# Attention grouped by half batches, and half of one batch's queries turned by the DMA

## The chip, the cores and the metric

The kernel runs on one core of a Trainium2 chip. The metric is the device time of one execution in microseconds. Engines are called by their names: TensorE (PE in the profile) multiplies matrices, VectorE (DVE) and ScalarE (ACT) work on tiles elementwise, GpSimd (POOL) and SyncE (SP) issue DMAs here.

## The reference

Linformer attention for 8 batches, 8 heads, 1024 tokens and head size 64, with keys and values projected to 64 rows, and then a maxout layer of two products on the 8192 tokens:

```python
k_proj = np.einsum('ks,bhsd->bhkd', E, k)
v_proj = np.einsum('ks,bhsd->bhkd', F, v)
scores = scale * np.matmul(q, k_proj.transpose(0, 1, 3, 2))
scores = scores - np.max(scores, axis=-1, keepdims=True)
attn = np.exp(scores)
attn = attn / (np.sum(attn, axis=-1, keepdims=True) + 1e-09)
attn_out = np.matmul(attn, v_proj)
x = attn_out.transpose(0, 2, 1, 3).reshape(B * S, H * D)
h1 = x @ w1
h2 = x @ w2
g = np.maximum(h1, h2)
return (g @ w_out).astype(np.float32)
```

w1 and w2 are 512x1024, w_out is 1024x512.

## The kernel before

**Units.** A unit is half a batch: 512 tokens, all 512 features; there are two for each of 8 batches, numbered n = 0 to 15 in the order in which they are done. The layer on a unit has up products (L745: x times a difference of weights, then a relu on the result, the tile gt_sb) and down products (L837: gt_sb and x times output weights). Both are made with seven block products in place of eight, so VectorE forms sums of blocks first (L705, the tiles that the profile calls big). In the main loop the seven up products of unit n+1 (p1, p2, p6, p5, p7, p3, p4, for two passes d = 0 and 1) alternate on TensorE with pieces of the down products of unit n. ScalarE copies most results out of their bank (`keep`, L719), and VectorE adds others (L760), then takes the relu (L763).

**The order** is written out by hand. A list `slots` holds the matmul pieces with keys, and `at_slot(key, step, ...)` puts further work behind one of them: `("P", n, p, i)` is piece i of down product p of unit n; `("U", n, h, i)` is up product i of half h of unit n (h is the pass d); `("G", n, h)` is the place at the head of half h. Each engine works through its instructions in the order in which the loop emits them.

**Attention** of a batch is done in four groups: two halves of the tokens (j) times two groups of four heads (g). A group has scores (16 small matmuls on tiles of 64x32, L340), their exp (ScalarE, into ex_sb), sums of the exps (8 matmuls by ones, L352) and values (16 matmuls, L352), the log and the exp of minus the log of the sums (ScalarE, ld_sb: the inverse), and the product of values and inverse (VectorE, into xt_sb, which is x of the layer). In the steady state `step_group` at `("G", n, h)` does the scores of the next group into banks mm2 and mm3, then sums and values of the group before (`step_da`) in the two double banks called att. The exps (two of 128x512), the log, the inverse and one product of 128x1024 (L499) follow in that half of the unit, so each half of a unit has one product. `step_later` puts log, inverse and product into slots `U(n, h, 0)` to `U(n, h, 2)`.

The sums of the exps are tested once per inverse: `check` (L396) lets SP write a few rows of ld_sb to a tile.

**Batch 1** is started in the down products of unit 0, by a string of names with one slot each: kv and kpt are projections of k and v, qt00 to qt11 turn q on TensorE (8 transposes each, L311, with a copy out by VectorE, L316), sc00 and sc10 are scores, dn and in sums and inverses, at and AT values and products. The key `("P", n // 15, (n - 1) // 2 % 7, (n - 1) % 2)` maps the place in the string to a piece.

**Later batches** have their q turned by DMA_TRANSPOSE from SP (`step_qt_dma`, L323) in two halves by heads. `step_gate` makes GpSimd's next loads wait for it. Batch 2 has its projections of k and v in unit 1 (`step_kv_sets`, `step_kpt_sets`), batches 3 to 7 in the units n = 3, 5, 7, 9 and 11 (`kv_units`; `step_kv` at `G(n, 0)`, L195, with the copies L205 to L212 by VectorE).

Of the kernel before, what the change touches and what calls it, by code (L numbers as in the profile page):

```python
# [19 lines left out]
def kernel(  # L20
# [12 lines left out]
    nc = tc.nc  # L33
# [272 lines left out]
    def step_qt(t, h0, nh=2, i0=0, i1=NI, att=False):  # L306
        qt_ps = att_banks(FP16)[:, 0, :] if att else mm_bank(FP16)
        ni = i1 - i0
        for h in range(nh):
            for i in range(ni):  # L310
                nc.tensor.transpose(  # L311
                    out=qt_ps[:, (h * ni + i) * 128 : (h * ni + i + 1) * 128],
                    in_=t["q"][:, h0 + h, 2 * (i0 + i) : 2 * (i0 + i) + 2, :],
                    identity=ident16,
                )
        nc.vector.tensor_copy(  # L316
            out=t["qt"][:, h0 : h0 + nh, i0 * 128 : i1 * 128],
            in_=qt_ps[:, 0 : nh * ni * 128].rearrange("q (h n) -> q h n", h=nh),
        )


    def step_qt_dma(t, h0=0, h1=H):
        nc.sync.dma_start_transpose(  # L323
# [6 lines left out]
    W = HALF // 2  # L330
    Z = D // 2

    def score(t, g, j, banks):
        for h in range(2):
            for o in range(2):
                for e in range(2):
                    head = 4 * g + 2 * h + e
                    for s in range(2):
                        pos = D * (o ^ e) + s * Z
                        nc.tensor.matmul(  # L340
                            out=banks[e][pos : pos + Z, h * W : (h + 1) * W],
                            lhsT=kpt_of(t, head, o)[:, s * Z : (s + 1) * Z],
                            rhs=t["qt"][o * D : (o + 1) * D, head, j * W : (j + 1) * W],
                            start=True, stop=True,
                        )
        t["ex", g, j] = soft.tile([128, 2, HALF], FP16, tag="soft", name="ex_sb")
# [24 lines left out]

    def x_out(t, g, j):
        return t["xt"][:, 2 * g : 2 * g + 2, :, j * W : (j + 1) * W]
# [74 lines left out]
            )  # L448


    def step_group(ln_later, t, g, j, t2, g2, j2):
        def new():
            if t is None:
                return lambda: None
            banks = [mm_bank(n=2 + e) for e in range(2)]
            score(t, g, j, banks)
            return lambda: scores(t, g, j, banks)

        if t2 is None:
            new()()  # L460
            t_later[0] = None
        else:
            first = (g, j) == (0, 0) and t is not tiles[2]
            acts = None if first else new()
            t_later[0] = step_da(t2, g2, j2, lambda: (new() if first else acts)(), ln_later)

    def scores(t, g, j, banks):
        for e in t["first"]:
            nc.scalar.activation(  # L469
                out=t["ex", g, j][:, e, :], in_=banks[e], func=ACTF.Exp, scale=scale  # L470
            )

    t_later = [None]

    def step_later():
        if t_later[0] is not None:
            t_later[0] = t_later[0]()

    def step_da(t, g, j, between, ln_later):
        if "xt" not in t:  # L480
            new_xt(t)
        dn_ps = att_banks()[:, :, 0:W]
        at_ps = att_banks()
        sums_into(t, g, j, dn_ps)
        values_into(t, g, j, [at_ps[:, o, :] for o in range(2)])
        between()
        ld = soft.tile([128, 2, W], FP32, tag="soft", name="ld_sb")

        def ln():
            nc.scalar.activation(out=ld, in_=dn_ps, func=ACTF.Ln)  # L490
            return invert

        def invert():
            nc.scalar.activation(out=ld, in_=ld, func=ACTF.Exp, scale=-1.0)
            check(ld)
            return finish

        def finish():
            nc.vector.tensor_tensor(  # L499
                out=x_out(t, g, j).rearrange("q z o n -> q o z n"),  # L500
                in0=at_ps.rearrange("q o (z n) -> q o z n", z=2),
                in1=ld[:, :, None, :].broadcast_to([128, 2, 2, W]),
                op=ALU.mult,
            )

        return ln if ln_later else ln()

# [505 lines left out]
    def loads(b, *names):  # L1013
        for n in names:
            b_ = b + (n == "k" and b < 2)
            if (b_, n) == (1, "q"):
                alloc(tiles[1], "q")
                for c in (0, NC // 2):
                    nc.gpsimd.dma_start(
                        out=tiles[1]["q"][:, :, c : c + NC // 2],  # L1020
                        in_=q[1].rearrange("h (p c) d -> p h c d", c=NC)[:, :, c : c + NC // 2],
                    )
# [59 lines left out]
    at_slot((0, 22), new_attn, t)  # L1082
    at_slot((0, 22), lambda: turn.__setitem__(slice(None), [2, 3]))
    for n, x in enumerate((
        "", "", "", "", "", "kv", "", "kpt", "qt00 qt10", "", "sc00 sc10", "qt01",
        "qt11 dn00 in00 dn10 in10", "", "", "at00 AT10 sc01",
    )):
        key = ("P", n // 15, (n - 1) // 2 % 7, (n - 1) % 2) if n else (0, 22)
        for name in x.split():
            if name[0] == "k":  # L1090
                if name == "kpt":
                    at_slot(key, step_kpt_sets, t)
                else:
                    at_slot(key, step_kv_sets, t)
                    at_slot(key, loads, 2, "v", "q")
            else:
                g, j = int(name[2]), int(name[3])
                s_ = {"qt": step_qt, "sc": step_sc,
                      "dn": step_dn, "in": step_inv, "at": step_at, "AT": step_at}[name[:2]]
                args = (4 * g, 4, 2 * j, 2 * j + 2) if name[:2] == "qt" else (g, j)  # L1100
                at_slot(key, s_, t, *args, *([True] if name[:2] == "AT" else []))
        if n in (1, 5):
            at_slot(key, step_t, 1, (0, 1) if n == 1 else (2, 3))
        if n in (2, 3):
            for i in range(2):
                at_slot(key, step_tw, 2 * (n - 2) + i)
        if 6 <= n < 10:
            at_slot(key, sums_x, U[0, 1], ((2, 0, 1, 3)[n - 6],))
# [1 line left out]

    t = tiles[2]
    at_slot(("P", 0, 2, 0), new_attn, t)
    at_slot(("P", 0, 2, 0), step_qt_dma, t, 0, H // 2)
    at_slot(("U", 1, 0, 1), step_kv_sets, t)
    at_slot(("U", 1, 0, 4), step_kpt_sets, t)
    at_slot(("P", 0, 6, 0), step_qt_dma, t, H // 2, H)
    at_slot(("U", 1, 0, 6), step_gate, t, "qt", H // 2 - 1)
    at_slot(("U", 1, 0, 6), loads, 3, "k", "v", "q")
# [12 lines left out]
        at_slot(("U", n, 0, 6), loads, b + 1, "k", "v", "q")  # L1131
    for n, h in (3, 1), (4, 0), (4, 1), (5, 1), (6, 0), (6, 1), (7, 1), (8, 0):
        at_slot(("U", n, h, 3), lambda: held.pop(0)())
    groups = [(tiles[b], g, j) for b in range(1, B) for j in range(2) for g in range(2)][2:]
    none = (None, None, None)
    for i, (new, old) in enumerate(zip([*groups[1:], none], groups)):
        n, h = divmod(i + 2, 2)
        if new[0] is not None:
            at_slot(("G", n, h), lambda t=new[0], h=h: t.__setitem__("first", (h, 1 - h)))
        ln_later = (n, h) == (1, 1) or h == 0 and n in kv_units  # L1140
        at_slot(("G", n, h), step_group, ln_later, *new, *old)
        at_slot(("U", n, h, 0), step_later)
        if ln_later:
            at_slot(("U", n, h, 1), step_later)
        at_slot(("U", n, h, 2), step_later)

    for n, (b, o) in enumerate(units):
        u = U[b, o]
# [215 lines left out]
```

## Time and profile before

| | |
|---|---|
| median of 3 runs | 320.2 us (320.08 to 320.25) |
| profiled execution: span | 318.1 us |
| profiled execution: time | about 320.2 us, some 2.1 us of it around the span |
| granted TensorE clock | 1.000 |
| TensorE busy | 312.3 us, 3922 matmuls |
| VectorE busy | 241.1 us, 441 instructions |
| ScalarE busy | 206.2 us, 373 instructions |
| HBM read, written | 57.15 MB, 16.78 MB |

In a row of the timeline the first number is the start in us after the start of the span, the second how long the instruction (or the x instructions of the row, which overlap) took; matmuls are pipelined, so the time from one start to the next is what one costs. In brackets stands for how long the engine had been idle and what ended that. A row of waits has the total in us, the number of times and the longest. In the lists of 40 digits each digit is the busy share of 1/40 of the span in tenths.

### The profile page before, as it was taken

The numbers are of one execution on the slowest core, as the hardware profiler recorded it, in microseconds if no ns is written. First come the engines' busy times: TensorE is split into PE (matmuls) and PEld (weight loads), VectorE is DVE, ScalarE is ACT, GpSimd is POOL, SyncE is SP. The second block draws the span as 40 slices with busy tenths as digits, with TensorE's granted clock in tenths as the row PEclk, the third lists the DMA queues.
The fourth block names the chain that finished last, engine by engine and source line by source line (L and its number), as shares of the span: only waits on it lengthen the run. The fifth ranks groups of instructions, "written<-read, shape, count | busy, mean of one in ns | idle before, by whom it ended". The sixth has DMA issues, their size and how long they took to land.

```text
span 318.1 us, 9308 instructions
## 1 busy us (share of the span) xinstructions
PE 312.3 (98%) x3922; PEld 253.6 (80%) x3922; DVE 241.1 (76%) x441; ACT 206.2 (65%) x373; POOL 40.8 (13%) x63
## 2 busy tenths in 40 slices
PE   8989999999999999999999999999999999999996
PEld 3555588888887888788887888788887888888885
DVE  2366888877969696996969696996969696969883
ACT  2476842777776777477776778477776777765541
POOL 8259002003000300022000400030000000000000
PEclk9999999999999999999999999999999999999999
DMA  7999999999979999899999999989979131313124
GB/s 189 206 200 195 207 206 202 207 158 160 204 139 195 162 212 245 210 182 154 223 233 217 167 204 245 215 151 183 232 149 209 45 102 36 102 35 102 36 99 136
DMA packets 76684, 53.71 MB, mean 169 GB/s; under 512 B 29664, under 2 KB 76128, under 8 KB 76640
## 3 DMA queue, kind: packets, MB, share of 16 engines
q0 software_dynamic: 30688, 28.05, 56.0%
q1 hardware_dynamic: 45664, 24.85, 32.7%
q8 instruction: 31, 0.51, 0.6%
q10 hardware_dynamic: 288, 0.20, 0.2%
q14 instruction: 13, 0.11, 0.1%
HBM read 57.15 MB, written 16.78 MB: 232 GB/s over the span
## 4 chain that ended last, share of the span: by engine, by line
PE 92%; DMA 5%; POOL 1%; ACT 1%; issue 0%; DVE 0%; POOLq 0%
PE mm_ps L837 47%; PE mm_ps L745 27%; PE mm_ps L524 4%; DMA v_sb<-in_v_dram 4%; PE att_ps L352 3%; PE mm_ps L195 3%; PE mm_ps L340 2%; PE mm_ps L633 2%; PE att_ps L237 1%; DMA out_dram<-o_sb 1%; PE mm_ps L311 1%; POOL k_sb L108 0%; POOL q_sb L108 0%; ACT ld_sb L388 0%; ACT ex_sb L380 0%
## 5 line engine op out<-in xcount | busy, mean ns | idle before, releaser
L719 ACT COPY p_sb<-mm_ps 128x512 f32<-128x512 f32 x179 | 101.8, 592 | 49.1 <-PE mm_ps L745 27.2
L837 PEld LDWEIGHTS <-big 128*128 128x128 f16 x768 | 73.5, 98 | 11.8 <-issue 3.6
L837 PE MATMUL mm_ps<-T_sb,big 128*128 128x256 f16 x576 | 76.9, 273 | 0.0
L760 DVE TENSOR_TENSOR gt_sb<-mm_ps,p_sb 128x512 f16<-128x512 f32 x56 | 38.5, 687 | 43.0 <-PE mm_ps L745 41.6
L745 PE MATMUL mm_ps<-big,big 128*128 128x256 f16 x336 | 50.4, 273 | 0.0
L745 PEld LDWEIGHTS <-big 128*128 128x128 f16 x448 | 43.8, 98 | 5.1
L837 PE MATMUL mm_ps<-wo_sb,gt_sb 128*128 128x256 f16 x256 | 42.6, 273 | 0.0
L837 PEld LDWEIGHTS <-gt_sb 128*128 128x128 f16 x376 | 35.7, 98 | 6.7 <-issue 2.7
L469 ACT ACTIVATE ex_sb<-mm_ps 128x512 f16<-128x512 f32 x50 | 27.2, 596 | 18.0 <-PE mm_ps L340 12.3
L745 PEld LDWEIGHTS <-wd_sb 128*128 128x128 f16 x336 | 32.9, 98 | 3.8
L745 PE MATMUL mm_ps<-xt_sb,wd_sb 128*128 128x256 f16 x224 | 32.8, 273 | 0.0
L499 DVE TENSOR_TENSOR xt_sb<-att_ps,ld_sb 128x1024 f16<-128x1024 f32 x26 | 31.7, 1219 | 0.2
L837 PE MATMUL mm_ps<-m_sb,xt_sb 128*128 128x256 f16 x128 | 24.4, 273 | 0.0
L303 POOL COPY junk<-qt_sb 1x1 f16<-1x1 f16 x6 | 2.1, 346 | 172.5 <-DMA qt_sb<-q_sb 172.5
L868 DVE TENSOR_TENSOR o_sb<-mm_ps,p_sb 128x512 f32<-128x512 f32 x32 | 21.9, 683 | 2.8 <-ACT p_sb L897 2.0
L763 DVE TENSOR_SCALAR gt_sb<-gt_sb 128x512 f16<-128x512 f16 (+1 forms) x60 | 20.9, 348 | 2.1
L705 DVE TENSOR_TENSOR big<-gt_sb 128x1024 f16<-128x1024 f16 x32 | 21.8, 683 | 0.0
L837 PE MATMUL mm_ps<-wo_sb,big 128*128 128x256 f16 x128 | 21.5, 273 | 0.0
L806 ACT ACTIVATE gt_sb<-mm_ps 128x512 f16<-128x512 f32 x28 | 16.8, 601 | 5.7 <-PE mm_ps L745 5.7
L837 PE MATMUL mm_ps<-T_sb,gt_sb 128*128 128x256 f16 x120 | 20.3, 273 | 0.0
L837 PEld LDWEIGHTS <-xt_sb 128*128 128x128 f16 x188 | 18.3, 98 | 2.3 <-issue 0.2
L760 DVE TENSOR_TENSOR gt_sb<-p_sb 128x512 f16<-128x512 f32 x28 | 19.1, 682 | 0.6 <-ACT p_sb L719 0.6
(121 smaller groups left out, 434.7 us busy)
## 6 DMA issues: line engine op xcount, KB each, us to landing
out_dram<-o_sb SPq DMA_DIRECT2D x62, 256.0 KB
k_sb<-in_k_dram POOLq DMA_DIRECT2D x7, 1024.0 KB, 9.8
v_sb<-in_v_dram POOLq DMA_DIRECT2D x7, 1024.0 KB, 15.3
q_sb<-in_q_dram POOLq DMA_DIRECT2D x5, 1024.0 KB, 23.0
q_sb<-in_q_dram POOLq DMA_DIRECT2D x6, 512.0 KB, 15.8
big<-in_moe_w_dram POOLq DMA_DIRECT2D x12, 128.0 KB, 6.3
v_sb<-in_v_dram POOLq DMA_DIRECT2D x4, 256.0 KB, 13.6
wo_sb<-in_moe_w_out_dram POOLq DMA_DIRECT2D x1, 1024.0 KB, 10.4
```

What stands on the lines that cost most here:

```text
L195: nc.tensor.matmul(out=kv_ps[r * KP : (r + 1) * KP, h * D : (h + nh) * D], lhsT=eft[i][:, c, :], rhs=t[w][:, h0 + h : h0 + h + nh, c, :], ...
L469: nc.scalar.activation(out=t["ex", g, j][:, e, :], in_=banks[e], func=ACTF.Exp, scale=scale)
L499: nc.vector.tensor_tensor(out=x_out(t, g, j).rearrange("q z o n -> q o z n"), in0=at_ps.rearrange("q o (z n) -> q o z n", z=2), in1=ld[:, ...
L524: nc.tensor.matmul(out=h_ps, lhsT=wd_sb[:, r, fb * 128 : (fb + 1) * 128], rhs=t["xt"][:, r, :, j * W : (j + 1) * W], start=(r == 0), stop= ...
L705: nc.vector.tensor_tensor(out=S(i), in0=S(0) if x is None else x, in1=y(), op=op)
L719: copy(out=x, in_=bank)
L745: nc.tensor.matmul(out=bank[:, m * W : (m + 1) * W], lhsT=w_[:, n_, (2 * d + m) * 128 : (2 * d + m + 1) * 128], rhs=a[:, n_, :], start=(n ...
L760: nc.vector.tensor_tensor(out=c_blk(j, c), in0=two(x), in1=two(y), op=ALU.add)
L763: nc.vector.tensor_scalar_max(ap, ap, 0.0)
L806: nc.scalar.activation(out=out, in_=in_, func=ACTF.Relu)
L837: nc.tensor.matmul(out=bank[i][:, 0:CH] if two_banks else bank[:, i * CH : (i + 1) * CH], lhsT=a(c)[:, i * 128 : (i + 1) * 128], rhs=w_(c) ...
L868: nc.vector.tensor_tensor(out=o_sb, in0=two(x), in1=two(y), op=ALU.add)
```

## The change

Attention of batches 1 to 7 goes by half batches (j) instead of groups. `pair_scores` at `G(n, 0)` makes the scores of both groups of heads in the two att double banks; `pair_exp` at `U(n, 0, 1)` and `U(n, 0, 2)` takes one exp of 128x1024 for each group of heads; `pair_values` at `G(n, 1)` makes the sums of both groups in mm2 and mm3 (one bank for each half o of the tokens) and the values in the att banks, with the two logs; `pair_inv` and `pair_mult` follow for o = 1 and o = 0 in `U(n, 1, 0)` to `U(n, 1, 2)`, the product in four pieces of 128x512. The k and v work of batch 2 moves from `U(1, 0, 1)` and `U(1, 0, 4)` to `U(1, 0, 5)` and `U(1, 1, 4)`, and the DMA turn of the first half of its q from `P(0, 2, 0)` to `P(0, 6, 0)`.

Batch 1's q is laid out by halves of the tokens (`halves`); its first half is turned on TensorE as before (qt00, qt10), its second half by one DMA_TRANSPOSE (`qd`, in the slot of qt00 and qt10) in place of qt01 and qt11. Its scores for the second half move from the end of the string to `G(1, 0)`.

The diff, cut:

```diff
+    def halves(t, n):
+        flat = t[n].rearrange("p h c d -> p (h c d)" if n == "q" else "p h n -> p (h n)")
+        return flat.rearrange("p (j h n) -> p j h n", j=2, h=H)
+
+    def step_qt_half_dma(t, j):
+        nc.sync.dma_start_transpose(
+            out=halves(t, "qt")[:, j].rearrange("q h (i p) -> q (h i) p", p=128),
+            in_=halves(t, "q")[:, j].rearrange("p h n -> p (h n)"),
+        )
...
-    def step_group(ln_later, t, g, j, t2, g2, j2):
-    def scores(t, g, j, banks):
-    def step_later():
-    def step_da(t, g, j, between, ln_later):
...
+    pair = {}
+
+    def pair_scores(t, j):
+        banks = pair["sc"] = [att_banks() for _ in range(2)]
+        for g in range(2):
+            score(t, g, j, [banks[g][:, e, :] for e in range(2)])
+
+    def pair_exp(t, j, g):
+        nc.scalar.activation(out=t["ex", g, j], in_=pair["sc"][g], func=ACTF.Exp, scale=scale)
+
+    def pair_values(t, j, order):
+        if "xt" not in t:
+            new_xt(t)
+        dn_ps = [mm_bank(n=2 + o) for o in range(2)]
+        at_ps = pair["at"] = [att_banks() for _ in range(2)]
+        for g in range(2):
+            tiles_into(
+                lambda o: dn_ps[o][:, g * W : (g + 1) * W], t["ex", g, j],
+                lambda rows, hh: ones16[rows, 0:Z],
+            )
+        for g in range(2):
+            values_into(t, g, j, [at_ps[g][:, o, :] for o in range(2)])
+        pair["ld"] = [soft.tile([128, 2, W], FP32, tag="soft", name="ld_sb") for _ in range(2)]
+        for o in order:
+            nc.scalar.activation(
+                out=pair["ld"][o].rearrange("p g w -> p (g w)"), in_=dn_ps[o], func=ACTF.Ln
+            )
+
+    def pair_inv(o):
+        ld = pair["ld"][o]
+        nc.scalar.activation(out=ld, in_=ld, func=ACTF.Exp, scale=-1.0)
+        check(ld)
+
+    def pair_mult(t, j, o):
+        for g in range(2):
             nc.vector.tensor_tensor(
-                out=x_out(t, g, j).rearrange("q z o n -> q o z n"),
-                in0=at_ps.rearrange("q o (z n) -> q o z n", z=2),
-                in1=ld[:, :, None, :].broadcast_to([128, 2, 2, W]),
+                out=x_out(t, g, j)[:, :, o, :],
+                in0=pair["at"][g][:, o, :].rearrange("q (z n) -> q z n", z=2),
+                in1=pair["ld"][o][:, g, None, :].broadcast_to([128, 2, W]),
                 op=ALU.mult,
             )
...
-        "", "", "", "", "", "kv", "", "kpt", "qt00 qt10", "", "sc00 sc10", "qt01",
-        "qt11 dn00 in00 dn10 in10", "", "", "at00 AT10 sc01",
+        "", "", "", "", "", "kv", "", "kpt", "qt00 qt10 qd", "", "scores", "",
+        "values", "", "", "mult",
...
-    at_slot(("P", 0, 2, 0), step_qt_dma, t, 0, H // 2)
-    at_slot(("U", 1, 0, 1), step_kv_sets, t)
-    at_slot(("U", 1, 0, 4), step_kpt_sets, t)
+    at_slot(("U", 1, 0, 5), step_kv_sets, t)
+    at_slot(("U", 1, 1, 4), step_kpt_sets, t)
+    at_slot(("P", 0, 6, 0), step_qt_dma, t, 0, H // 2)
...
+    for n in range(1, last - 1):
+        t, j = tiles[(n + 2) // 2], n % 2
+        at_slot(("G", n, 0), pair_scores, t, j)
+        for g in range(2):
+            at_slot(("U", n, 0, g + 1), pair_exp, t, j, g)
+        at_slot(("G", n, 1), pair_values, t, j, (1, 0))
+        for i, o in enumerate((1, 0)):
+            at_slot(("U", n, 1, i), pair_inv, o)
+            at_slot(("U", n, 1, i + 1), pair_mult, t, j, o)
```

More of the change, by code (lines that the diff above doesn't have):

```diff
@@ L310, in step_qt @@
             for i in range(ni):
+                if t is tiles[1]:
+                    block = halves(t, "q")[:, i0 // ni, h0 + h, i * 128 : (i + 1) * 128]
+                else:
+                    block = t["q"][:, h0 + h, 2 * (i0 + i) : 2 * (i0 + i) + 2, :]
                 nc.tensor.transpose(
                     out=qt_ps[:, (h * ni + i) * 128 : (h * ni + i + 1) * 128],
-                    in_=t["q"][:, h0 + h, 2 * (i0 + i) : 2 * (i0 + i) + 2, :],
-                    identity=ident16,
+                    in_=block, identity=ident16,
                 )
         nc.vector.tensor_copy(
-            out=t["qt"][:, h0 : h0 + nh, i0 * 128 : i1 * 128],
+            out=halves(t, "qt")[:, i0 // ni, h0 : h0 + nh] if t is tiles[1]
+            else t["qt"][:, h0 : h0 + nh, i0 * 128 : i1 * 128],
             in_=qt_ps[:, 0 : nh * ni * 128].rearrange("q (h n) -> q h n", h=nh),
+        )
[6 more added lines that the diff above has]
+            in_=halves(t, "q")[:, j].rearrange("p h n -> p (h n)"),
         )
@@ L331, with qt_of @@
     Z = D // 2
+    def qt_of(t, head, j):
+        if t is tiles[1]:
+            return halves(t, "qt")[:, j, head]
+        return t["qt"][:, head, j * W : (j + 1) * W]
     def score(t, g, j, banks):
@@ L342, in score @@
                             lhsT=kpt_of(t, head, o)[:, s * Z : (s + 1) * Z],
-                            rhs=t["qt"][o * D : (o + 1) * D, head, j * W : (j + 1) * W],
+                            rhs=qt_of(t, head, j)[o * D : (o + 1) * D],
                             start=True, stop=True,
@@ L448, in step_at @@
             )
-    def step_group(ln_later, t, g, j, t2, g2, j2):
[L452 to L465, printed above, removed]
@@ L467, in scores @@
-    def scores(t, g, j, banks):
[L468 to L473, printed above, removed]
-    def step_later():
-        if t_later[0] is not None:
-            t_later[0] = t_later[0]()
-    def step_da(t, g, j, between, ln_later):
+    pair = {}
[3 more added lines that the diff above has]
+            score(t, g, j, [banks[g][:, e, :] for e in range(2)])
@@ L480, in step_da @@
+    def pair_exp(t, j, g):
+        nc.scalar.activation(out=t["ex", g, j], in_=pair["sc"][g], func=ACTF.Exp, scale=scale)
+    def pair_values(t, j, order):
         if "xt" not in t:
             new_xt(t)
[L482 to L498, printed above, removed]
+        dn_ps = [mm_bank(n=2 + o) for o in range(2)]
[7 more added lines that the diff above has]
+            values_into(t, g, j, [at_ps[g][:, o, :] for o in range(2)])
@@ L501, in finish @@
-                in0=at_ps.rearrange("q o (z n) -> q o z n", z=2),
-                in1=ld[:, :, None, :].broadcast_to([128, 2, 2, W]),
+                out=x_out(t, g, j)[:, :, o, :],
+                in0=pair["at"][g][:, o, :].rearrange("q (z n) -> q z n", z=2),
+                in1=pair["ld"][o][:, g, None, :].broadcast_to([128, 2, W]),
                 op=ALU.mult,
             )
-        return ln if ln_later else ln()
     wd_sb = const.tile([128, NDC, DF], FP16)
@@ L1017, in loads @@
                 alloc(tiles[1], "q")
-                for c in (0, NC // 2):
+                for j in range(2):
                     nc.gpsimd.dma_start(
-                        out=tiles[1]["q"][:, :, c : c + NC // 2],
-                        in_=q[1].rearrange("h (p c) d -> p h c d", c=NC)[:, :, c : c + NC // 2],
+                        out=halves(tiles[1], "q")[:, j].rearrange("p h (c d) -> p h c d", d=D),
+                        in_=q[1].rearrange("h (p c) d -> p h c d", c=NC)[:, :, j * NI : (j + 1) * NI],
                     )
@@ L1095 @@
                     at_slot(key, loads, 2, "v", "q")
-            else:
[L1097 to L1101, printed above, removed]
+            elif name[:2] == "qt":
+                g, j = int(name[2]), int(name[3])
+                at_slot(key, step_qt, t, 4 * g, 4, 2 * j, 2 * j + 2)
+            elif name == "qd":
+                at_slot(key, step_qt_half_dma, t, 1)
+            elif name == "scores":
+                at_slot(key, pair_scores, t, 0)
+                for g in range(2):
+                    at_slot(key, pair_exp, t, 0, g)
+            elif name == "values":
+                at_slot(key, pair_values, t, 0, (0, 1))
+                for o in range(2):
+                    at_slot(key, pair_inv, o)
+            else:
+                for o in range(2):
+                    at_slot(key, pair_mult, t, 0, o)
         if n in (1, 5):
@@ L1133 @@
         at_slot(("U", n, h, 3), lambda: held.pop(0)())
[L1134 to L1145, printed above, removed]
+    for n in range(1, last - 1):
+        t, j = tiles[(n + 2) // 2], n % 2
+        at_slot(("G", n, 0), pair_scores, t, j)
+        for g in range(2):
+            at_slot(("U", n, 0, g + 1), pair_exp, t, j, g)
[3 more added lines that the diff above has]
+            at_slot(("U", n, 1, i + 1), pair_mult, t, j, o)
     for n, (b, o) in enumerate(units):
```

## The prediction

> **What bounds the kernel now.** The page comes first, then the waits of TensorE, then the timelines of stages that the change touches.
>
> ```profile
> span 318.1 us, 9308 instructions
> PE 312.3 (98%) x3922; PEld 253.6 (80%) x3922; DVE 241.1 (76%) x441; ACT 206.2 (65%) x373; POOL 40.8 (13%) x63
> ...
> DVE  2366888877969696996969696996969696969883
> ...
> PEclk9999999999999999999999999999999999999999
> DMA  7999999999979999899999999989979131313124
> ...
> PE 92%; DMA 5%; POOL 1%; ACT 1%; issue 0%; DVE 0%; POOLq 0%
> ```
>
> TensorE is busy for 98% of the span at an undiminished clock and is 92% of the chain that ended last. So one microsecond less of matmuls is one microsecond less of time, as long as nothing new makes TensorE wait, and any new wait counts in full. The line of VectorE's tenths is the one to keep in mind: from slice 13 on it mostly goes 9, 6, 9, 6. A slice is 8 us, near the length of half a unit, so VectorE has full stretches and slack ones, although its mean is 76%. The waits of the engines say the same:
>
> ```profile
> PE att_ps L352 <- ACT ex_sb L380: 0.3, 1, 0.3
> ...
> DVE gt_sb L760 <- PE mm_ps L745: 41.6, 22, 3.0
> ```
>
> TensorE's list has no wait that recurs with the units (the largest of one that belongs to attention is this 0.3 us, once). VectorE's idle time is 22 waits of up to 3 us for the first sum of an up product, that is, in one place per half and not spread out.
>
> The time of a run is the span of 318.1 us and about 2.1 us around it; the median is 320.2. I take the sum of changes in the span and add it to 320.2. A measurement of this kernel can tell about 0.2%, or 0.64 us, from no change.
>
> **Batch 1 on TensorE: what goes.** First TensorE, then ScalarE, in the stretch where batch 1 is started.
>
> ```profile
> 52.58 1.06 PE L311 MATMUL mm_ps<-ident,q_sb 128*128 128x128 f16 x16
> 53.48 1.47 PE L837 MATMUL mm_ps<-T_sb,big 128*128 128x256 f16 x12
> 54.88 0.63 PE L340 MATMUL att_ps<-qt_sb,kpt_sb 64*32 64x256 f16 x32
> 55.44 0.61 PE L837 MATMUL mm_ps<-wo_sb,big 128*128 128x256 f16 x4
> ...
> 57.21 0.61 PE L311 MATMUL mm_ps<-ident,q_sb 128*128 128x128 f16 x8
> 57.75 0.41 PE L352 MATMUL att_ps<-ex_sb,ones 64*32 64x256 f16 x16
> ...
> 63.01 0.41 PE L340 MATMUL mm_ps<-qt_sb,kpt_sb 64*32 64x256 f16 x16
> 63.24 0.29 PE L352 MATMUL att_ps<-ex_sb,ones 64*32 64x256 f16 x8
> 63.35 0.40 PE L352 MATMUL att_ps<-ex_sb,vp_sb 64*32 64x256 f16 x16
> ```
>
> ```profile
> 55.47 1.95 ACT L380 ACTIVATE ex_sb<-att_ps 128x1024 f16<-128x1024 f32 x2
> ```
>
> Sixteen transposes take 0.90 us start to start (52.58 to 53.48); qt01 and qt11, 8 each, go to the DMA: -0.89. The small tiles run in rounds of eight: 8 sums take 0.11 (63.24 to 63.35), 32 scores 0.44. The block of 32 scores takes 0.56 until the next full matmul, and 0.09 before it (twelve matmuls of 0.109 end at 54.79): about 0.21 for a block by itself. Batch 1 has four such blocks before and three after (scores; sums with values; G(1,0)): -0.21. Later units have two before and two after, with the same number of rounds. TensorE thus loses **1.1 us** of work.
>
> Half of that comes back at once. The exps of the first half batch end at 55.47 + 1.95 = 57.42, and the sums begin at 57.75, with 0.33 to spare. Without the two blocks of transposes between them the sums are due at 56.86, those of the second group, which need the second exp, at 56.97: a wait of 0.45, with the signal about **0.5 us**.
>
> **The four mults in one half.** This is the part that I hold decisive. Before, each half of a unit has one product with the inverse, 128x1024, on VectorE. After, the same products are done by four of 128x512, all in the second half of the unit, ahead of the same sums.
>
> ```profile
> 61.81 1.28 DVE L443 TENSOR_TENSOR xt_sb<-att_ps,ld_sb 128x512 f16<-128x512 f32 x2
> ...
> 111.70 1.22 DVE L499 TENSOR_TENSOR xt_sb<-att_ps,ld_sb 128x1024 f16<-128x1024 f32 x1
> 112.83 0.68 DVE L868 TENSOR_TENSOR o_sb<-mm_ps,p_sb 128x512 f32<-128x512 f32 x1
> ...
> 116.14 0.43 DVE L763 TENSOR_SCALAR gt_sb<-gt_sb 128x1024 f16<-128x1024 f16 x1
> ```
>
> ```profile
> 115.83 0.41 PE L340 MATMUL mm_ps<-qt_sb,kpt_sb 64*32 64x256 f16 x16
> ...
> 116.94 0.60 PE L837 MATMUL mm_ps<-wo_sb,gt_sb 128*128 128x256 f16 x4
> ```
>
> One mult of 1024 holds VectorE for 1.13 (111.70 to 112.83). Two of 512 take 1.28 together, the second starting 0.60 after the first, so four hold it for 2.40. VectorE works without a gap from 111.70 to beyond 116.57, so its later work in the second half is 1.27 us later. The relu of 116.14 ends at 116.57 before, at 117.84 after. Its first reader is the third of the four matmuls of 116.94 (the second pass of the up product wrote blocks 2 and 3 of that half of gt_sb), which is due at 117.16. TensorE gets there 0.11 earlier, since the block at the head of the next unit has four rounds of scores instead of five of all kinds. So what had 0.6 to spare now waits 117.84 - 117.05 = **0.79**, in six places: ahead of units 4, 6, 8, 10, 12 and 13.
>
> Ahead of units 3, 5, 7, 9 and 11 the k and v sums come in between and something else is late first:
>
> ```profile
> 98.14 0.69 DVE L705 TENSOR_TENSOR big<-gt_sb 128x1024 f16<-128x1024 f16 x1
> 99.02 0.68 DVE L205 CAST kp_sb<-mm_ps 64x512 f16<-64x512 f32 x1 [0.20 <-PE mm_ps L195]
> 99.73 0.70 DVE L210 CAST vp_sb<-mm_ps 64x512 f16<-64x512 f32 x1
> ```
>
> ```profile
> 100.98 0.60 PE L837 MATMUL mm_ps<-wo_sb,gt_sb 128*128 128x256 f16 x4
> ```
>
> Here VectorE has 0.2 idle, and the casts start 1.0 later (after 98.14 + 0.69 + 1.27, less the overlap of 0.08). The cast of v, which empties the bank that the matmuls of 100.98 write, ends at 101.43 instead of 100.43; TensorE is due at 100.87. It waits about **0.6**, five times. Ahead of unit 14, the last place of this kind:
>
> ```profile
> 291.06 0.29 DVE L763 TENSOR_SCALAR gt_sb<-gt_sb 128x512 f16<-128x512 f16 x1
> ```
>
> ```profile
> 291.69 0.60 PE L837 MATMUL mm_ps<-wo_sb,gt_sb 128*128 128x256 f16 x4
> ```
>
> The relu would end at 292.62; the third matmul is due at 291.91: **0.7**. The waits don't grow from unit to unit, since the first half of each unit loses its mult of 1.13 and VectorE catches up there. That half had slack anyway (the 3.0 us of the waits above), so nothing is gained by it.
>
> **The rest.** ScalarE gets two exps of 1024 for four of 512, starts them in the first half, and has the same count of logs and inverses; at 65% and with no wait of TensorE for it in the units I take 0, with 0 to 0.1 us per unit as bounds (0 to 1.3). The k and v work of batch 2 moves by half a unit, and its copy to the score layout now waits for an attention bank that the mults empty: 0 to 0.5, I take 0. The place ahead of unit 2 could have one more wait of 0.8; I take 0, because the VectorE work of batch 2 around it moves too.
>
> **The turned half batch.** It is issued by SP as soon as the second half of batch 1's q has landed, and is first read in G(1,0).
>
> ```profile
> q_sb<-in_q_dram POOLq DMA_DIRECT2D x2, 512.0 KB, 20.9
> ```
>
> ```profile
> 65.91 2.99 SPq L323 DMA_TRANSPOSE qt_sb<-q_sb  x1
> ```
>
> ```profile
> 71.52 0.18 POOL L303 COPY junk<-qt_sb 1x1 f16<-1x1 f16 x1 [19.27 <-DMA qt_sb<-q_sb]
> ```
>
> ```profile
> DMA to landing us min/median/max: 15.1/15.8/16.5
> ```
>
> The two halves of q were issued from 29.95 us on and landed 20.9 later at the median; the transposes of 52.58 wait for nothing, so the second half is there at about 52.5. G(1,0) moves from 63.01 to 63.01 - 1.1 + 0.5 - 0.22 (the scores that now lie in it and not before it) = 62.2. A turn of the same size, half of batch 2's q, was issued at 65.91 and had landed by 71.5: 5.6 us, so 58.1 at the earliest, and TensorE doesn't wait. But at 52 to 62 the DMA engines are full with k, v and q (the row of nines). At the other end it comes after all that is queued: q of batch 2 was issued from 50.76 on and landed after 15.1 to 16.5, at about 67; with 3 us for the turn itself 70, and TensorE waits 7.8. If the 2.99 us of the turn are doubled by sharing evenly in time, it lands at 61.1. I take that one, in time by 1 us, as the row of 65.91 itself ran beside the end of such a load, and keep the far end for a rival. Behind it on SP are the checks of the inverses and the two turns of batch 2, which are first read a unit later; nobody waits for these.
>
> [...] No row before shows a turn in the midst of loads.
>
> **The sum.** -1.1 + 0.5 + 6 x 0.79 + 5 x 0.6 + 0.7 = +7.8 us: **328.0 us**, 2.4% slower. Each of the twelve places in VectorE's part may be off by 0.3 (3.6 in all); with the bounds of the rest 324.4 to 333.
>
> **The rivals.** *The turn is late on top of this.* For it: the full DMA row, and loads of k, v and q queued ahead. Against it: the 5.6 us of the row above. It decides from a landing after 62.2; the price is up to 7.8, in the middle 4: about 332 us. *The mults don't hold TensorE, and the change wins.* This needs VectorE to be late by less than 0.5 instead of 1.27 in the second half, for instance if one pair of mults ran in the up to 3.0 us in which VectorE waits for the first sum of an up product. Then only batch 1's saving and its wait are left: 320.2 - 1.1 + 0.5 = 319.6, or 319.1 without the wait. For it: VectorE has 24% idle, and ScalarE has less to do. Against it: the first pair is placed behind the relu of that product, in an engine that works in order. *Only part of the waits comes*, because each place has more spare time than its row shows: half of 7.8 is left, some 323. [...]
>
> **How the numbers follow.** VectorE's waits with the turn in time: 0.48 (324.4 to 331). With the turn late: 0.31 (330 to 335). Part of the waits: 0.09 (320.5 to 324.4). No waits, faster: 0.10 (319.0 to 319.8). Slow turn: 0.02. The range 323.0 to 333.5 leaves out the faster case, half of the partial one, the upper end of the late turn and the slow turn, about 2 in 10. Faster by over 0.2% has 0.10, slower by over 0.2% the rest but for 0.03 in between, at the low edge of the partial case.
>
> **What would show it.** In the profile after, TensorE's list of waits should have rows for VectorE's relu of gt_sb (some 7 times, 0.6 to 0.9 each) and for the cast of v (5 times), VectorE's mults should stand four in a row for 2.4 us, and the scores of G(1,0) should start at about 62.2. A wait there for qt_sb from the DMA is the first rival. If TensorE has no wait by units, the step on the mults is wrong, and with it the forecast. If L352 of batch 1 begins at 56.9 without a wait, the term of 0.5 is wrong.

## The result, and the profile after

The changed kernel takes 342.04 us (median of 5, 341.19 to 342.37) against 320.2: 1.068 times as long, with a 95% interval of 1.0667 to 1.0693. I had forecast 328.0 and a range to 333.5. The page of the changed kernel:

```profile
span 340.3 us, 9269 instructions
PE 316.4 (93%) x3906; PEld 252.8 (74%) x3906; DVE 242.1 (71%) x465; ACT 202.5 (60%) x348; POOL 39.7 (12%) x63
...
PEclk9999999859999999999999999999999999999999
DMA  8999999999921999799995999699959420212023
...
PE 50%; DVE 27%; DMA 17%; issue 3%; POOL 1%; ACT 1%; DVEq 0%; POOLq 0%
```

TensorE has 16 matmuls fewer and yet 4 us more of busy time, its clock has a hole in slices 8 and 9, and the chain that was 92% TensorE now runs through VectorE for 27% and the DMA for 17%. TensorE's list of waits says where (what TensorE was to write and its line, what it waited for, us in all, times, longest):

```profile
PE att_ps L359 <- DMA qt_sb<-q_sb: 10.2, 1, 10.2
PE mm_ps L841 <- DVE gt_sb L767: 4.6, 7, 0.7
PE mm_ps L841 <- DVE vp_sb L210: 2.1, 5, 0.4
...
PE att_ps L260 <- DVE xt_sb L505: 0.4, 1, 0.4
PE mm_ps L371 <- ACT ex_sb L478: 0.3, 1, 0.3
```

The rows 2 and 3 are those that I had looked for: the relu seven times, the cast of v five times. The first is the turn, and larger than I allowed.

The list makes each wait too short. It counts from the end of the matmul before, and a single one of these is 0.27 us long while the next can start 0.11 after it. From start to start a wait costs 0.16 more than its entry. One place of the cast and one of the relu:

```profile
112.01 1.04 PE L749 MATMUL mm_ps<-xt_sb,wd_sb 128*128 128x256 f16 x8
113.46 0.61 PE L841 MATMUL mm_ps<-wo_sb,gt_sb 128*128 128x256 f16 x4 [0.42 <-DVE vp_sb L210]
...
129.49 0.38 PE L841 MATMUL mm_ps<-wo_sb,gt_sb 128*128 128x256 f16 x2
130.53 0.39 PE L841 MATMUL mm_ps<-wo_sb,gt_sb 128*128 128x256 f16 x2 [0.66 <-DVE gt_sb L767]
```

Behind the eight matmuls from 112.01 on the next could start at 112.88, behind the two from 129.49 on at 129.70, so the waits cost 0.58 and 0.83. All twelve places together cost 5 x 0.58 + 7 x 0.83 = 8.7 us.

How late the work is can be read by the same up product in both timelines. Before, and after:

```profile
71.13 0.60 PE L745 MATMUL mm_ps<-xt_sb,big 128*128 128x256 f16 x4
```

```profile
82.24 0.61 PE L749 MATMUL mm_ps<-xt_sb,big 128*128 128x256 f16 x4
```

It is 11.1 us late in unit 1. Near the end of the main loop the first matmul of one such product is at 294.74 before and at 316.66 after:

```profile
294.74 0.49 PE L745 MATMUL mm_ps<-big,big 128*128 128x256 f16 x3
```

```profile
316.66 0.60 PE L749 MATMUL mm_ps<-big,big 128*128 128x256 f16 x4
```

That is 21.9. So half of the loss lies at the start of batch 1 and half is collected in the units behind it. The start is shown in TensorE's timeline and in a table of stretches. A row of the table has the stretch, its length, the busy us of PE, PEld (TensorE's loading of weights), DVE, ACT and POOL with their instructions, then the granted clock, the DMA's share (packets overlap, so it can be above 1) and GB/s:

```profile
61.91 0.38 PE L841 MATMUL mm_ps<-m_sb,xt_sb 128*128 128x256 f16 x2
72.46 1.05 PE L359 MATMUL att_ps<-qt_sb,kpt_sb 64*32 64x256 f16 x32 [10.17 <-DMA qt_sb<-q_sb]
...
76.67 0.60 PE L841 MATMUL mm_ps<-T_sb,big 128*128 128x256 f16 x4
```

```profile
64.00:66.00 2.00, 0.00 (x0) 0.00 (x0) 0.42 (x2) 0.00 (x0) 0.00 (x0) 1.00 1.21 196
66.00:67.00 1.00, 0.00 (x0) 0.00 (x0) 0.00 (x0) 0.00 (x0) 0.00 (x0) 0.63 1.19 191
...
74.00:76.00 2.00, 2.00 (x12) 1.39 (x11) 0.00 (x0) 0.62 (x2) 0.18 (x1) 0.50 1.11 96
76.00:77.00 1.00, 1.00 (x8) 0.82 (x7) 0.06 (x1) 0.89 (x1) 0.70 (x1) 0.75 1.04 232
77.00:78.00 1.00, 1.00 (x12) 0.89 (x10) 0.97 (x3) 0.69 (x2) 0.18 (x1) 1.00 0.11 7
```

TensorE stands still from 62.3 to 72.4. The granted clock falls from 1.00 to 0.50 at about 66.3, four microseconds into the wait, and is back at 1.00 at about 76.5, four after the work is (worked out from the 0.63 of 66 to 67 us and the 0.75 of 76 to 77).

Why the turn is late is seen in the queues between 62 and 70 us (packets, MB, and the time of the packets as a share of the 16 engines' time):

```profile
q0 software_dynamic: 1247, 1.24, 91.3%
q1 hardware_dynamic: 1245, 0.32, 29.8%
```

The loads (q0) and the turn (q1) move packet for packet, 1247 and 1245, but a load's packet has 1 KB and the turn's 256 B. The turn gets a quarter of the packet time (29.8 of 121.1%), some 155 packets a microsecond. No run here shows how many packets are taken from one queue at a time.

### The profile page after: what moved, and what is told of

It is laid out like the page before. It is cut to its first block, busy times and chain, and to the rows that moved or that the text cites. A ratio compares the mean times of both kernels' runs of the same rounds, so it can differ in the third digit from the quotient of the medians.

```text
span 340.3 us, 9269 instructions
## 1 busy us (share of the span) xinstructions
PE 316.4 (93%) x3906; PEld 252.8 (74%) x3906; DVE 242.1 (71%) x465; ACT 202.5 (60%) x348; POOL 39.7 (12%) x63
## 4 chain that ended last, share of the span: by engine, by line
PE 50%; DVE 27%; DMA 17%; issue 3%; POOL 1%; ACT 1%; DVEq 0%; POOLq 0%
PE mm_ps L841 28%; PE mm_ps L749 16%; DVE xt_sb L505 9%; DVE gt_sb L764 7%; DMA q_sb<-in_q_dram 6%; DMA qt_sb<-q_sb 6%; DVE o_sb L872 4%; DMA v_sb<-in_v_dram 4%; DVE big L709 2%; PE att_ps L371 2%; DVE gt_sb L767 2%; PE mm_ps L528 2%; PE mm_ps L371 1%; DVE vp_sb L210 1%; DVE kp_sb L205 1%
## 5 line engine op out<-in xcount | busy, mean ns | idle before, releaser
L723 ACT COPY p_sb<-mm_ps 128x512 f32<-128x512 f32 x179 | 100.9, 592 | 92.6 <-PE mm_ps L841 49.9
L841 PE MATMUL mm_ps<-T_sb,big 128*128 128x256 f16 x576 | 77.8, 275 | 0.0
L841 PE MATMUL mm_ps<-wo_sb,gt_sb 128*128 128x256 f16 x256 | 43.9, 273 | 6.7 <-DVE gt_sb L767 4.6
L841 PEld LDWEIGHTS <-gt_sb 128*128 128x128 f16 x376 | 34.7, 98 | 16.5 <-DVE gt_sb L767 6.5
L505 DVE TENSOR_TENSOR xt_sb<-att_ps,ld_sb 128x512 f16<-128x512 f32 x56 | 34.7, 680 | 0.0
L749 PE MATMUL mm_ps<-xt_sb,wd_sb 128*128 128x256 f16 x224 | 33.5, 277 | 0.0
L478 ACT ACTIVATE ex_sb<-att_ps 128x1024 f16<-128x1024 f32 x28 | 28.8, 1032 | 0.0
L872 DVE TENSOR_TENSOR o_sb<-mm_ps,p_sb 128x512 f32<-128x512 f32 x32 | 21.9, 683 | 4.7 <-PE mm_ps L841 4.6
L303 POOL COPY junk<-qt_sb 1x1 f16<-1x1 f16 x6 | 1.1, 177 | 192.9 <-DMA qt_sb<-q_sb 192.9
L709 DVE TENSOR_TENSOR big<-gt_sb 128x1024 f16<-128x1024 f16 x32 | 21.8, 682 | 0.0
L359 PE MATMUL att_ps<-qt_sb,kpt_sb 64*32 64x256 f16 x512 | 10.9, 280 | 10.3 <-DMA qt_sb<-q_sb 10.2
```

Of the source, the lines that this page charges most:

```text
L359: nc.tensor.matmul(out=banks[e][pos : pos + Z, h * W : (h + 1) * W], lhsT=kpt_of(t, head, o)[:, s * Z : (s + 1) * Z], rhs=qt_of(t, head, j ...
L478: nc.scalar.activation(out=t["ex", g, j], in_=pair["sc"][g], func=ACTF.Exp, scale=scale)
L505: nc.vector.tensor_tensor(out=x_out(t, g, j)[:, :, o, :], in0=pair["at"][g][:, o, :].rearrange("q (z n) -> q z n", z=2), in1=pair["ld"][o] ...
L709: nc.vector.tensor_tensor(out=S(i), in0=S(0) if x is None else x, in1=y(), op=op)
L723: copy(out=x, in_=bank)
L749: nc.tensor.matmul(out=bank[:, m * W : (m + 1) * W], lhsT=w_[:, n_, (2 * d + m) * 128 : (2 * d + m + 1) * 128], rhs=a[:, n_, :], start=(n ...
```

## The experiments

Two theories are tested, one for each half of the loss: the turn shares the engines packet for packet and makes TensorE wait and then run slowly; the four mults in the second half make the units wait. Rivals: the turn is slow by itself; the units' waits are an after-effect of the late start.

**Turn on TensorE, grouping kept.**

```diff
-        "", "", "", "", "", "kv", "", "kpt", "qt00 qt10 qd", "", "scores", "",
-        "values", "", "", "mult",
+        "", "", "", "", "", "kv", "", "kpt", "qt00 qt10", "", "scores", "qt01",
+        "qt11 values", "", "", "mult",
```

> The changed kernel with both halves of batch 1's q turned on TensorE, the grouping kept. Theory (the turn shares the DMA engines packet for packet with the loads and comes 10 us late; the units' waits of 0.6 to 0.7 us come from the four mults in the second half): the wait of 10.2 us and the slow clock behind it (about 2 us) go, 16 transposes and one short block come back (+0.9 to 1.1), the units' waits stay: 330 to 331.5 us. Rival (the units' waits are an after-effect of the late start of batch 1): 320 to 322 us.

Measured: 332.37 us (the kernel before, run beside it: 319.94). The clock is 1.0 all along, and the units' waits are the same as with the late start:

```profile
PE mm_ps L841 <- DVE gt_sb L767: 4.6, 7, 0.7
PE mm_ps L841 <- DVE vp_sb L210: 2.1, 5, 0.4
...
PE mm_ps L371 <- DVE qt_sb L319: 1.4, 1, 1.4
```

The rival of the after-effect falls. The third row accounts for the 0.9 us above the expected range: the sums now use the banks from which VectorE copies the turned q, and wait 1.4 for it. Without this wait the grouping costs some 11 us; against this version the turn by the DMA costs some 9.7.

**Turn by the DMA, grouping of before.** All of the turn's code is put into the kernel before; in place of the string's end:

```diff
-        "", "", "", "", "", "kv", "", "kpt", "qt00 qt10", "", "sc00 sc10", "qt01",
-        "qt11 dn00 in00 dn10 in10", "", "", "at00 AT10 sc01",
+        "", "", "", "", "", "kv", "", "kpt", "qt00 qt10 qd", "", "sc00 sc10", "",
+        "dn00 in00 dn10 in10", "", "", "at00 AT10 sc01",
```

> The kernel before with only the second half of batch 1's q turned by the DMA; attention stays in groups. Theory: the scores that read it are due near 59.5 us, earlier than in the changed kernel, and wait until about 72 us: 12.5 us, then some 2 us of slow clock, less 0.9 for the transposes: about 334 us, no recurring wait on VectorE in the units. Rival (a late start makes the units wait for VectorE): 334 plus up to 9 us, with such waits in the units.

Measured: 335.3 us at the median of two runs (334.44 and 336.16), a wait of 12.9 us, no recurring waits. The size is near the expected one, but not for the reason given. SP's timeline:

```profile
65.53 3.05 SPq L337 DMA_TRANSPOSE qt_sb<-q_sb  x1
68.77 1.82 SPq L331 DMA_TRANSPOSE qt_sb<-q_sb  x1
```

The first row is batch 2's turn, which in the kernel before stands ahead on SP and waits for its own load; batch 1's turn was issued only behind it, at 68.8. The change had moved batch 2's turn, and I had left that out. Repeated with that move:

```diff
-    at_slot(("P", 0, 2, 0), step_qt_dma, t, 0, H // 2)
+    at_slot(("P", 0, 6, 0), step_qt_dma, t, 0, H // 2)
```

> The kernel before with only the second half of batch 1's q turned by the DMA, and with the turns of batch 2 behind it on SP (they stood ahead of it in the first version of this experiment, which was issued at 68.8 us instead of 52.7). Theory (packet for packet sharing with the loads): issued at 52.7, landed near 72 as in the changed kernel, a wait of 12 to 13 us, 334 to 335.5 us. Rival (in the changed kernel the turn was held up by something of the new grouping): it lands by 62 us, a wait of under 3 us, 320 to 323 us.

Measured: 334.45 us, a wait of 12.1. The turn was now issued at 52.77 and was still as late, without any of the new grouping. The up products of 71.13 and of 294.74 are both 14.3 us later than in the kernel before, so in the old grouping the late start costs nothing more in the units. SP's timeline:

```profile
52.77 8.34 SPq L331 DMA_TRANSPOSE qt_sb<-q_sb  x1
```

**Loads of batch 2 behind the turn.**

```diff
-                    at_slot(key, loads, 2, "v", "q")
...
                 at_slot(key, step_qt_half_dma, t, 1)
+                at_slot(key, step_gate, t, "qt", H // 2)
+                at_slot(key, loads, 2, "v", "q")
```

> The changed kernel with the loads of batch 2's v and q issued only when the turn has landed; only batch 2's k is still in the queue beside it. Theory (packet for packet sharing): the turn lands at 59 to 61.5 us instead of 72.3, TensorE doesn't wait or by under 0.5 us, the clock stays at 1.0; the time falls by about 12: 329.5 to 331 us, unless v and q of batch 2 come late in their turn. Rival (the turn is slow by itself, or by the new layout of q): it lands near 72 again and the time stays at 341 to 343.

Measured: 332.77 us at the median of two runs (331.63 and 333.9), the span of the profiled one 329.8, the clock 1.0. GpSimd's gate shows the landing:

```profile
61.42 0.18 POOL L303 COPY junk<-qt_sb 1x1 f16<-1x1 f16 x1 [28.94 <-DMA qt_sb<-q_sb]
```

The same turn of the same layout lands 11 us earlier when only the end of the load of batch 2's k is beside it. No load is in the queues from 58 to 61 us, and the turn's packets move three times as fast (482 a microsecond against 155):

```profile
q1 hardware_dynamic: 1446, 0.37, 112.1%
```

So it isn't slow by itself, and the packets beside it are the cause. The two runs are 0.6 and 2.9 us above the expected range. In the first, the profiled one, v of batch 2 now comes late (a wait of 1.0); for the second there is no trace.

**The mults of o = 1 early.** The inverse of o = 1 goes behind the logs, its two mults ahead of the first sum of the up products.

```diff
-            at_slot(("U", n, 1, i), pair_inv, o)
-            at_slot(("U", n, 1, i + 1), pair_mult, t, j, o)
+            at_slot(("U", n, 1, 1) if i else ("G", n, 1), pair_inv, o)
+            at_slot(("U", n, 1, 2 * i), pair_mult, t, j, o)
```

> The changed kernel with the inverse and the two mults of half o = 1 one slot earlier (inverse behind the logs, mults ahead of the first sum of the up products, where VectorE waits about 3 us); the DMA turn as it is. Theory: 1.2 of the 1.27 us by which VectorE is late fall into its idle time, the twelve waits of 0.4 to 0.7 us and the smaller ones go: 342 less 7 to 10.5: 331.5 to 335 us, the wait of 10.2 us stays. Rival (waits are an after-effect of the late start, or the bank casts are late by themselves): 340 to 342.

Measured: 333.38 us. The rows for the relu and the cast are gone from TensorE's waits; the turn's 10.0 is left. VectorE in one unit, in the changed kernel and with this edit:

```profile
123.42 0.69 DVE L764 TENSOR_TENSOR gt_sb<-mm_ps,p_sb 128x512 f16<-128x512 f32 x1 [3.34 <-PE mm_ps L749]
...
124.35 2.48 DVE L505 TENSOR_TENSOR xt_sb<-att_ps,ld_sb 128x512 f16<-128x512 f32 x4
```

```profile
121.53 1.29 DVE L505 TENSOR_TENSOR xt_sb<-att_ps,ld_sb 128x512 f16<-128x512 f32 x2 [1.75 <-ACT ld_sb L500]
122.99 0.69 DVE L764 TENSOR_TENSOR gt_sb<-mm_ps,p_sb 128x512 f16<-128x512 f32 x1 [0.17 <-PE mm_ps L749]
...
123.92 1.28 DVE L505 TENSOR_TENSOR xt_sb<-att_ps,ld_sb 128x512 f16<-128x512 f32 x2
```

The four mults hold VectorE for 2.40 us in the changed kernel (124.35 to 126.75), as the prediction had it. With two of them inside the 3.3 us in which VectorE waited anyway, the time is 8.7 us less, and 8.7 is what the twelve waits cost. It was their place, not their number.

**The wait filled with matmuls.** `fill` makes 44 matmuls of 128x512 into mm2, ahead of the waiting scores:

```diff
+        if n == 1:
+            at_slot(("G", n, 0), fill, 44)
         at_slot(("G", n, 0), pair_scores, t, j)
```

> The changed kernel with 44 matmuls of 128x512 without a reader (9.5 us) put ahead of the scores that wait for the turn, so that TensorE works while it waits. Theory (the idle 10 us lower the granted clock, and the slow clock costs about 2 us after the wait): the clock stays at 1.0 and the time falls to 339.5 to 340.6 us. Rival (the low clock is only a record, or the slow stretch behind the wait comes from the DMA's load): 341.5 us or more.

Measured: 341.29 us, clock 1.000 throughout. The time lies between the two expectations, but the rows separate the terms:

```profile
73.39 0.63 PE L359 MATMUL att_ps<-qt_sb,kpt_sb 64*32 64x256 f16 x32 [1.64 <-DMA qt_sb<-q_sb]
...
75.71 0.60 PE L848 MATMUL mm_ps<-T_sb,big 128*128 128x256 f16 x4
```

From the scores to the third group of four behind them it takes 2.32 here and 4.21 in the changed kernel (72.46 to 76.67): the slow clock cost 1.9 us. The turn was 0.9 later in this run, so 1.0 of the gain is left, and the medians show 0.75.

**Both repairs**, the loads behind the turn and the mults of o = 1 early:

> The changed kernel with both repairs: the mults of o = 1 early, and the loads of batch 2's v and q behind the turn. Theory (the two causes are separate and each repair takes its own away): left are 1.1 us of saved work, the wait for the exp (0.3), about 1.5 us of waits for batch 2's v, and 0.6 of small ones: 321.0 to 321.8 us, no wait for the turn, none for VectorE by units. Rival (the repairs hit the same time, or the mults' early slot only worked behind a late start): 323 to 330.

Measured: 322.35 us (before beside it 320.13; ratio 1.0072, interval 1.0039 to 1.0106), between the expected range and the rival's. The two causes add up: in the spans of the profiled runs the repairs take 10.5 and 8.9 us away alone and 19.6 together; in the medians they account for 19.7 of 21.8. A wait of 1.3 for v of batch 2 remains, and in the profiled run one of 1.6 for a load of k at the very beginning, which lies ahead of all that was changed.

**Both repairs, loads at the second exp of batch 1** (the gate reads ex_sb and not qt_sb):

> As the kernel with both repairs, but the loads of batch 2's v and q wait for the second exp of batch 1 (about 57.5 us) instead of for the turn's landing. Theory: GpSimd's issue and its 3 us until first packets let the turn finish alone at about 60 to 62 us, v of batch 2 comes 3 us earlier, its wait goes: 319.7 to 320.5 us. Rival (the loads catch up with the turn's packets): a wait for the turn of 1 us or more in the place of the other, 321 to 323.

Measured: 320.87 us; against the kernel before 1.0014, interval 0.9991 to 1.0038: no difference that can be told, though 0.4 above the expected range. There is no wait for the turn nor for v of batch 2, the clock is 1.0, and the scores of G(1,0) start at 62.18, as the prediction had it for a turn in time:

```profile
62.18 0.63 PE L359 MATMUL att_ps<-qt_sb,kpt_sb 64*32 64x256 f16 x32
```

Up to there it is 0.8 us ahead of the kernel before, and at the end of the up products 0.5 behind it. Part of this is work that comes later; the rest are small waits of up products for a copy by ScalarE (L723), which the list of waits leaves out because they are short. One in the middle of the kernel, where the next matmul could start at 263.89 behind the four from 263.45 on:

```profile
263.45 0.60 PE L841 MATMUL mm_ps<-T_sb,big 128*128 128x256 f16 x4
263.95 0.60 PE L749 MATMUL mm_ps<-big,wd_sb 128*128 128x256 f16 x4
```

The trace has one of 0.06 in each of twelve units and two of 0.2 in unit 1, 1.1 us in all.

**Turn on TensorE behind the values**, with the mults early (`"values", "qt01", "qt11", "mult"`):

> The changed kernel with the mults of o = 1 early and both halves of batch 1's q on TensorE, the second half's transposes behind the sums and values instead of ahead of them. Theory: no wait for a DMA, none for VectorE in the units; 0.2 us of work saved against the kernel before, 0.5 to 1 us of small waits: 320.3 to 321.2 us. Rival (the grouping has a further cost of its own in the units): 322 us or more.

Measured: 323.6 us (ratio 1.01, 1.0075 to 1.0125), above the expected range and in the rival's. The scores of batch 1 wait 1.5 us in all, since the copies of the turned q hold up on VectorE the mults that empty their banks. The units do have a cost of their own, as the rival said, but a small one: the waits for ScalarE's copies make 1.0 us here, as in the version of 320.87. The profiled run (325.8) also waits 2.1 for a load of k at the very beginning. The rest of the 3.5 us at the median is open:

```profile
PE att_ps L359 <- DVE xt_sb L505: 1.5, 2, 1.3
```

**Both exps in one slot**, on the version of 320.87, `U(n, 0, 1)` in place of `g + 1`:

> The kernel with both repairs and loads at the exp (320.9 us), with both exps of a half batch in the slot U(n, 0, 1). Theory (the rest of about 0.06 us per unit is p3 of the up products waiting for ScalarE's copy of p5, which stands behind the second exp): 12 times 0.06 goes: 320.0 to 320.4 us. Rival (the copy of p6 now comes late in its place): 320.7 us or more.

Measured: 321.9 us (ratio 1.006, 1.0045 to 1.0074): worse, as the rival had it. The exps now stand as 1.95 us of ScalarE in one piece ahead of copies that TensorE needs (ScalarE's timeline, then TensorE's list of waits):

```profile
118.67 1.95 ACT L478 ACTIVATE ex_sb<-att_ps 128x1024 f16<-128x1024 f32 x2
```

```profile
PE mm_ps L749 <- ACT p_sb L723: 0.4, 1, 0.4
```

From start to start the waits for these copies make 2.3 us instead of 1.1; the difference of 1.2 is about that of the two versions (1.0).

**Values between the sums**, on top of that: the values of the first group of heads directly behind its sums.

> As the one with both exps together, and the values of the first group of heads between the sums of the first and of the second group, so that the second sums of batch 1 are due 0.33 us later than the wait of 0.31 us for the second exp. Theory: that wait goes: 319.6 to 320.2 us, 0 to 0.2% faster than the kernel before. Rival (the logs come 0.22 us later for it and hold the copies behind them): no change against the one before, 320.2 us or more.

Measured: 321.8 us, the same within the interval (1.005 to 1.0078). TensorE's wait for the second exp has left the list. The profiled run is 0.3 us faster than that of the version before it, but it was already 0.3 us ahead at 45 us, before the attention of batch 1, so nothing is gained behind that point; where the removed wait went is open.

**The kernel before with an early turn**: groups as before, the turn by the DMA with batch 2's behind it, batch 2's loads at the second exp of batch 1, and sc01 1.7 us later.

> The kernel before, attention in groups as it was, with the second half of batch 1's q turned by the DMA, the turns of batch 2 behind it on SP, the loads of batch 2's v and q at the second exp of batch 1 (about 57.5 us), and the scores that read the turned half at about 61.2 us instead of 59.5. Theory (the turn is only late for the packets beside it, and the other loss lay in the grouping): it lands at about 61.3, no wait or one under 0.5 us, clock 1.0, no recurring waits; 0.9 less for 16 transposes, 0.2 more for a block by itself, up to 0.4 for the sums that follow: 319.3 to 320.0 us, 0 to 0.25% faster than before. Rival (v of batch 2, needed at 65.5 us in this kernel, comes late and gives it all back): 321 to 325 us.

Measured: 324.07 us (ratio 1.0137, 1.0114 to 1.016), in the rival's range. The turn of batch 1 is in time, but in this grouping batch 2 is needed earlier, and its late loads show:

```profile
PE mm_ps L359 <- DMA qt_sb<-q_sb: 1.5, 1, 1.5
...
PE att_ps L237 <- DMA v_sb<-in_v_dram: 0.9, 1, 0.9
```

The first row stands at 75.09 us and is batch 2's turn. The profiled run took 322.7; what the slower ones (up to 325.15) waited for isn't shown. No version tried is faster than the kernel before.

## Why the prediction was wrong, step by step

**The step that failed: the landing of the turn.** I put the two bounds at 58.1 and 70 us and chose 61.1, by "sharing evenly in time". The rows of 62 to 70 us show the engines shared evenly in packets (1247 and 1245), and with 256 B against 1 KB that left the turn a quarter of the packet time (29.8 of 121.1%). TensorE went on at 72.46 and had waited 10.2 us, where the sum has nothing. The even sharing in time was my estimate; the prediction itself says that no row before shows a turn in the midst of loads. The row of the near bound, the turn of 65.91, said nothing on it, since the loads beside it were ending.

Even the near bound was too early. With v and q of batch 2 held back, the turn landed 8.6 us after its issue (52.85 to 61.42) and not 5.6. It is chance that this landing is so close to the 61.1 of the prediction. In the changed kernel the turn's first packets started at 56.7, 4.0 us after the issue of 52.74; those of the turn of 65.91 started at 67.2, 1.3 us after it was issued.

The rival of the late turn had the right cause, the loads, and was given 0.31, but its price was too small as well. I let the loads end at 67, as if the turn took nothing from them, so that the wait was 7.8 at most. With the turn beside them the last packets of the loads started at 71.8.

**The step that was missing: the clock.** The wait was priced as its length. The matmuls behind the wait of 10 us ran at a granted clock of 0.50 for 4 us, 1.9 us more. The clock of the kernel before was 1.000 with no wait of TensorE longer than 1.5 us, so its row of nines said nothing on a wait of 10.

**The mults: right, in mechanism and size.** From start to start the relu costs 0.83 seven times (I had 0.79 and 0.7) and the cast 0.58 five times (0.6). My sum for the twelve was 8.4, they cost 8.7, and taking the mults out of the way brought 8.7 in time.

**Small terms.** The wait for the second exp is 0.3 in the list and 0.5 from start to start, as forecast: of the two rounds of sums, which cost 0.11 each, the first starts at 56.90 and the second at 57.51.

```profile
56.90 0.30 PE L371 MATMUL mm_ps<-ex_sb,ones 64*32 64x256 f16 x8
57.51 0.30 PE L371 MATMUL mm_ps<-ex_sb,ones 64*32 64x256 f16 x8 [0.31 <-ACT ex_sb L478]
```

The saved 1.1 us holds too: with it and the 0.5 the scores of G(1,0) were to start at 62.2, and they start at 62.18 where the turn is in time. Two terms that I took as 0 were not: batch 2's copy to the score layout waits 0.4 (0.5 from start to start), and the copies of ScalarE cost 0.06 per unit, some 0.7 in the changed kernel. The first is at the upper bound that the prediction gave, the second inside.

The sum by the rows is -1.1 + 0.5 + 10.2 + 1.9 + 8.7 + 0.5 + 0.7 = 21.4 of the 21.8 us measured. The terms that the forecast had make 8.1 against its 7.8, so 12.1 of the 14.0 us by which it was off are the late turn and the slow clock behind it.

## What to carry to other kernels

Where a trace shows two queues taking packets one for one, as here, a DMA with small packets that runs beside queued loads with large ones should be priced by packets and not by time or bytes (256 B against 1 KB here, and a quarter of the packet time). If it is on the path, hold the loads back until it is nearly done, and look at who needs those loads next. Ask of each operation that moves between halves of a stage in which idle time of its engine it lies: VectorE had up to 3 us in a half to spare here, and the same mults cost 8.7 us on one side of that gap and next to nothing when two of them lay in it. The wait of 10 us of TensorE cost 1.9 us more than its length. Read the cost of a wait from start to start: the twelve waits for the mults make 6.7 us in the list and 8.7 in time.

## What the runs showed that I had not expected

That the turn and the loads move so exactly the same number of packets (1245 and 1247 in 8 us), and that the granted clock was 0.50 for the 4 us behind the wait of 10 us (1.9 us). In the kernel before neither could be seen: its turns ran when the loads were ending (from 68 to 69 us 870 packets of the turn and none of a load), and its clock was 1.000.
